# One stationary operand for two products in a recurrence kernel, and its odd heads two partition quarters away

## The chip, the cores and the metric

The kernel runs on one core of a Trainium2 chip. A core has TensorE (PE in the profile; its weight loads are listed as PEld), VectorE (DVE), ScalarE (ACT), GpSimd (POOL), SyncE (SP, which here only issues DMAs) and 16 DMA engines. Its on-chip memory has 128 partitions. TensorE is an array of 128x128; a matmul with a small operand can be placed on a part of it, called a square below: the row block is given by the partitions that the operands stand on, the column block by the partitions that the result goes to.

The metric is the device time of one execution in microseconds (us). All times below are in us where nothing else is said.

## The reference

The first half is a recurrence per batch and head over 768 time steps (4 batches, 8 heads, head size 40). The second half is a small network on the result: a matmul, x times cos(x), a matmul.

```python
for t in range(S):
    kt, vt, rt = (k[:, :, t], v[:, :, t], r[:, :, t])
    wt, at, bt = (w[:, :, t], a[:, :, t], b[:, :, t])
    y[:, :, t] = np.einsum('bhd,bhde->bhe', rt, state)
    Sa = np.einsum('bhde,bhe->bhd', state, at)
    state_decay = state * wt[:, :, None, :] - np.einsum('bhd,bhe->bhde', Sa, bt)
    state = state_decay + np.einsum('bhd,bhe->bhde', vt, kt)
...
h = x @ w_in          # (3072 x 320) @ (320 x 2048)
g = h * np.cos(h)
return g @ w_out      # (3072 x 2048) @ (2048 x 320)
```

## The kernel before, in words

**Tiling.** Time is cut into 24 chunks of 32 steps. 4 batches x 32 steps fill the 128 partitions: batch i of a chunk stands on partitions 32i to 32i+31, `blk[i]`, a quarter. Eight heads are handled as four pairs j with an even and an odd member e. Transposed operands (`aT`, `bT`, `kT`, `vT`, `rT`) hold the head dimension of an even head on partitions 0 to 39 and of an odd one on 64 to 103, `half[e]`.

**The recurrence in a chunk.** Within a chunk the steps are solved at once. Products of b (divided by the running decay) with a, masked to earlier steps, form a triangular 32x32 matrix per batch and head; its inverse is `rt`. Products of k (scaled alike) with a, masked with `su`, are `ag`. Products of v with r, plain and masked, go beside v into `vvm`. The state is kept in `qz`.

The work of a chunk is written as functions, each of which uses one or two PSUM buffers from a pool of two (`at`):
- ahead of the chunk, for pairs of chunks: `p1_w` (transposes w, makes the decays, divides b by w), `p1_a` (transposes and scales a), `p1_b` (transposes b of two chunks), `p1_n` (`nps`: the products of b with a of two chunks, 64 matmuls of 32 columns, then two copies by ACT into `nt`);
- for groups of four chunks, the inverse: a transpose on VectorE (line 486), 31 steps of two VectorE operations (lines 494 and 498) and a transpose back into `rt` (line 502), 33 entries in all;
- one chunk ahead: `p2_v` (transposes v and r), `p2_k` (transposes k), `p2_g` (`gram`: 32 matmuls for k with a, then 32 for v with r, then masks);
- the chain from chunk to chunk, called t, q, x, s, z: `ch_t` transposes the state, `ch_q` multiplies r with it, `ch_x` makes `x0ps` (32 matmuls of `ag` with `vvm`, then 32 of `aT` with `qz`), `ch_s` multiplies by the inverse (`sps`, 32 matmuls), `ch_z` makes `dps` from `kn` with `vvm` and from `bn` with the result of s, and brings the state up to date.

**Which squares these use.** In `ch_x` the first 32 matmuls of a chunk contract over quarter bb and write quarter bb ^ e: both members of every pair, eight different squares of 32x32. `ch_s` goes the other way round, on eight squares too. `p1_n` and `p2_g` use 64x32 parts, eight of them, `ch_q` four parts of 64x64, `ch_z` eight of 32x64.

**The second network** is cut into pieces for two chunks (256 tokens) and four blocks of the hidden layer. There are four kinds in turn: a and b of the first layer (`first_a`, `first_b`, tile `ph`) and two of the second layer (`second`, tile `po`). b ends in activations by ACT (lines 830 to 837) and products by VectorE (832, 840).

**Order.** Nothing is scheduled by a cost model: the order on every engine is the order in which the program issues. For each chunk a list `segs` names the functions and places M; at each M one piece of the second network is issued. Every element of the list, and every piece, is a step. With each step a counter of delayed work (`later(n, ...)`) runs down, by which DMAs, copies on POOL and the rest of the activations are issued n steps later, and one entry of the inverse is issued if any are waiting (`fill`). If the inverse is not complete when s comes up, more pieces are issued, each with four entries of the inverse, until it is. For chunk numbers that are 0, 1, 2 and 3 modulo 4 the lists are:

```python
segs = [t, v, M, q, M, k, x, M, g, M, s, pb, M, z, M, pn, M, M]
segs = [t, M, pw, q, M, x, k, M, s, v, M, z, M, pa, M, g, M, M]
segs = [t, M, pb, q, M, pn, v, M, x, M, s, k, M, g, M, z, M, M]
segs = [t, M, pw, q, M, x, k, M, s, v, M, z, M, pa, M, g, M, M]
```

The inverse for the next four chunks is put in the queue after pn of 2.

**DMA.** SP issues the loads of a chunk's inputs (four DMAs of 40 KB for each, `load`), the store of a chunk's result `xd`, and its return `xT` in the layout of the second network, three steps or more after z. SP's queue is in order.

Of the kernel before, what the change touches and what calls it, by code (L numbers as in the profile page):

```python
# [10 lines left out]
I32 = mybir.dt.int32  # L11
# [9 lines left out]
def kernel(  # L21
# [56 lines left out]
    every = slice(0, P)  # L78

# [114 lines left out]
    su = kept("su", [P, HH, C], 1, 1.0)[0]  # L194
    for i in range(4):
        nc.gpsimd.affine_select(
            su[blk[i]], su[blk[i]], pattern=[[0, HH], [1, C]], compare_op=ALU.is_gt, fill=0.0,
            base=0, channel_multiplier=-1,
        )
# [21 lines left out]
    WID = 512  # L221
    first_done, second_done = [], []

    def rounded(m, dst, src, by, by_sb):
# [16 lines left out]
        def taken():  # L241
            hi = t["words"][:, :, 1]
            t["mant"] = sb2.tile([P, WID], I32, tag="mant", name="mant")
            t["expo"] = sb2.tile([P, WID], I32, tag="expo", name="expo")
# [5 lines left out]
            t["sign"] = sb2.tile([P, WID], mybir.dt.bfloat16, tag="sign", name="sign")  # L250
# [142 lines left out]
    def over_w(c, wn):  # L393
        rw = ring.tile([P, H, D], F32, tag="rw", name="rw")
        nc.vector.reciprocal(rw, wn)  # L395
        nc.gpsimd.tensor_tensor(unpad(bn_b[c % 7]), unpad(nat["b", c]), rw, ALU.mult)  # L396
        G["rw", c] = rw

# [39 lines left out]
    def p1_n(c):  # L438
# [36 lines left out]
        if c % 4 == 2 and c > 2:  # L475
            inv_space()
# [115 lines left out]
    def p2_kn(c):  # L592
        nc.gpsimd.tensor_tensor(unpad(kn_b[c % 2]), nat["k", c], G["rw", c], ALU.mult)
        nc.gpsimd.tensor_copy(vvm[c % 2][:, :, C : C + D], nat["v", c])
        landed(c)
# [23 lines left out]
    def p2_g(c):  # L619
        kT, vT, aT, rT = G["kT"], G["vT"], G["aT", c], G["rT", c]  # L620
        ps = at("gram")
        for j in range(4):
# [6 lines left out]
        for j in range(4):  # L629
# [6 lines left out]
        ag = sb2.tile([P, H, C], F32, tag="ag", name="ag")  # L636
        nc.vector.tensor_tensor(
            ag.rearrange("p (e j) t -> p e (j t)", e=2), ps[:, :, : HH * C],
            su.rearrange("p j t -> p (j t)").unsqueeze(1).to_broadcast([P, 2, HH * C]), ALU.mult,
        )  # L640
        v1 = ps[:, :, HH * C : 2 * HH * C].rearrange("p e (j t) -> p e j t", t=C)
# [3 lines left out]
            su.unsqueeze(1).to_broadcast([P, 2, HH, C]), ALU.mult,  # L645
        )
        G["ag", c] = ag
# [28 lines left out]
    def ch_x(c):  # L676
        ps = at("x0ps")
        for j in range(4):
            o = C * (j // 2)
            for bb in range(B):  # L680
                for e in range(2):
                    mm(
                        ps[blk[bb ^ e], e, j * N72 : (j + 1) * N72], G["ag", c][blk[bb], 4 * e + j, :],
                        vvm[c % 2][blk[bb], 2 * j + e, o : o + N72], j == 0,
                    )
        if c:
            for j in range(4):
                o = (NZ - N72) * (j // 2)
                for bb in range(B):
                    for e in range(2):  # L690
                        mm(
                            ps[blk[bb ^ e], e, j * N72 : (j + 1) * N72],
# [480 lines left out]
```

## Time and profile before

| | |
|---|---|
| median of 3 runs | 800.21 (799.5 to 800.78) |
| profiled execution, its own time | 800.58 |
| its span | 798.9 |
| VectorE, time in the inverse's steps (lines 494 and 498) | 48.5 and 51.2 |
| POOL, of which the products kn (line 593) and bn (line 396) | 22.7 and 19.9 |
| DMA, mean over the span | 70 GB/s |
| TensorE idle, largest entries: wn for a scan by VectorE, bT for bn, wT for a load | 5.3, 4.9, 4.2 |

The waits in the last row lie in the first third of the execution. A row of the order in time gives start, duration, engine, line, operation, output and inputs, the tile shape of a matmul, the shape of the moving operand and how many instructions were merged. All matmuls from the helper `mm` show line 101, so they are told apart by their tiles. A duration of a merged row of matmuls includes the latency of the last one; the time that a block holds TensorE is read from its start to the next block's start.

### The profile page before, as it was taken

To read this page: it belongs to the slowest core of one execution; us is meant where nothing else is said; L and a number is where in the kernel's file an instruction comes from. 1 tells how busy PE (TensorE), PEld (TensorE's weight loads), DVE (VectorE), ACT (ScalarE), POOL (GpSimd) and SP (SyncE) were. 2 spreads that over 40 slices of the span, in tenths; PEclk is the share of its full clock that TensorE was granted. 3 is DMA by queue.
4 is the path that set the end of the run, shared out by engine and by line. 5 is a ranking of instruction groups with operands and counts; after the bars stand their busy time and mean duration, and the time that the engine had idled before them with its cause. 6 is when DMAs were issued, how large, how long until landed. Compare 5 with 4: busy or idle time off the path is not lost.

```text
span 798.9 us, 39602 instructions
## 1 busy us (share of the span) xinstructions
PE 745.9 (93%) x17812; PEld 571.0 (71%) x17812; DVE 486.7 (61%) x1025; ACT 383.4 (48%) x723; POOL 199.9 (25%) x354
## 2 busy tenths in 40 slices
PE   4768798999999999999999999999999999999997
PEld 4535576777766777777777787777787777777775
DVE  8768858864734896554895645994346863323331
ACT  1336567564435436545535635534545445354352
POOL 5326635230321330330330230332031122201000
PEclk9888899999999999999999999999999999999999
DMA  8575563343353314334214324223220222001000
GB/s 112 150 187 140 146 152 88 60 124 64 59 122 64 67 36 65 72 99 70 60 38 66 93 43 73 46 49 68 43 46 21 46 46 55 19 18 32 20 17 16
DMA packets 183304, 55.79 MB, mean 70 GB/s; under 512 B 157152, under 2 KB 178656, under 8 KB 183136
## 3 DMA queue, kind: packets, MB, share of 16 engines
q1 hardware_dynamic: 177440, 52.11, 30.6%
q8 instruction: 140, 2.29, 1.2%
q10 hardware_dynamic: 5440, 0.82, 0.8%
q0 software_dynamic: 256, 0.33, 0.3%
q14 instruction: 28, 0.23, 0.1%
HBM read 42.07 MB, written 11.14 MB: 67 GB/s over the span
## 4 chain that ended last, share of the span: by engine, by line
PE 65%; DVE 14%; DMA 5%; ACT 5%; issue 4%; POOL 3%; SPq 2%; DVEq 0%; ACTq 0%; POOLq 0%
PE ph L101 22%; PE po L101 20%; PE x0ps L101 3%; PE dps L101 3%; PE gram L101 3%; DVE rw L395 3%; PE vT L330 2%; PE sps L101 2%; PE qps L101 2%; PE nps L101 2%; DVE inv_tmp L494 2%; DVE inv L498 2%; DVE mant L245 1%; SPq L152 1%; PE kT L330 1%
## 5 line engine op out<-in xcount | busy, mean ns | idle before, releaser
L101 PE MATMUL po<-w_out_sb,gT 128*128 128x320 f32 x768 | 223.5, 439 | 0.1
L101 PE MATMUL ph<-xT,w_in_sb 128*128 128x256 f32 x768 | 185.7, 386 | 0.1
L101 PEld LDWEIGHTS po<-w_out_sb,gT 128*128 128x128 f32 x768 | 140.2, 190 | 54.6 <-issue 2.3
L101 PEld LDWEIGHTS ph<-xT,w_in_sb 128*128 128x128 f32 x768 | 139.3, 190 | 29.7 <-issue 12.4
L830 ACT ACTIVATE turns<-ph,rnd 128x512 f32<-128x512 f32 x96 | 64.1, 685 | 156.3 <-PE ph L101 155.9
L832 DVE SCALAR_TENSOR_TENSOR turns<-turns,ph 128x512 f32<-128x512 f32 x96 | 64.0, 683 | 109.4 <-ACT turns L830 109.2
L840 DVE TENSOR_TENSOR gT<-ph,turns 128x512 f32<-128x512 f32 x96 | 65.8, 686 | 38.4 <-ACT turns L837 38.4
L756 POOL TENSOR_TENSOR qz<-qz,wc 128x160 f32<-128x160 f32 x92 | 41.9, 475 | 168.5 <-DVE qz L755 167.9
L837 ACT ACTIVATE turns<-turns,half_pi 128x512 f32<-128x512 f32 x96 | 69.3, 722 | 3.1
L836 ACT ACTIVATE turns<-turns 128x512 f32<-128x512 f32 x96 | 60.1, 626 | 19.0 <-DVE turns L832 19.0
L101 PE MATMUL ph<-xT,w_in_tail 64*128 64x256 f32 (+1 forms) x512 | 54.6, 394 | 1.6 <-issue 1.6
L498 DVE TENSOR_TENSOR inv<-inv,inv_tmp 128x31 f32<-128x31 f32 (+15 forms) x124 | 51.2, 413 | 4.3
L755 DVE TENSOR_TENSOR qz<-dps,qz 128x160 f32<-128x160 f32 x92 | 28.9, 314 | 37.6 <-PE dps L101 37.3
L586 POOL COPY vp<-nat_v 128x320 f32<-128x320 f32 x24 | 11.7, 487 | 159.9 <-DMA nat_v<-in_v_dram 139.6
L494 DVE TENSOR_TENSOR inv_tmp<-u,inv 128x31 f32<-128x31 f32 (+15 forms) x124 | 48.5, 391 | 2.3
L395 DVE RECIPROCAL rw<-nat_w 128x320 f32<-128x320 f32 x20 | 42.8, 2142 | 0.1
L101 PEld LDWEIGHTS ph<-xT,w_in_tail 64*128 64x128 f32 (+1 forms) x512 | 32.2, 160 | 10.8 <-issue 7.3
L767 POOL TENSOR_TENSOR yt<-yt,wb 128x512 f32<-128x512 f32 x24 | 31.6, 1318 | 22.1 <-DVE yt L762 22.1
L659 ACT COPY s<-sT 104x416 f32<-104x416 f32 x46 | 20.8, 503 | 33.1 <-PE sT L655 33.1
L719 DVE TENSOR_TENSOR sm<-sps,su 128x128 f32<-128x128 f32 x48 | 11.7, 285 | 33.1 <-ACT sm L714 30.3
L396 POOL TENSOR_TENSOR bn<-nat_b,rw 128x320 f32<-128x320 f32 x22 | 19.9, 905 | 44.3 <-DVE rw L395 44.2
L671 ACT COPY qz<-qps 40x512 f32<-40x512 f32 x46 | 26.6, 579 | 6.8 <-PE qps L101 6.4
(136 smaller groups left out, 1100.3 us busy)
## 6 DMA issues: line engine op xcount, KB each, us to landing
words<-in_moe_w_in_dram SPq DMA_DIRECT2D x8, 512.0 KB
xd<-yt SPq DMA_DIRECT2D x48, 80.0 KB
out_dram<-ot SPq DMA_DIRECT2D x24, 160.0 KB
nat_k<-in_k_dram SPq DMA_DIRECT2D x92, 40.0 KB
nat_v<-in_v_dram SPq DMA_DIRECT2D x92, 40.0 KB
nat_r<-in_r_dram SPq DMA_DIRECT2D x92, 40.0 KB
nat_a<-in_a_dram SPq DMA_DIRECT2D x84, 40.0 KB
ws<-in_w_dram SPq DMA_DIRECT2D x5, 640.0 KB
```

The lines of the kernel that those rows point to most:

```text
L101: nc.tensor.matmul(o, lhsT=lhsT, rhs=rhs, start=start, stop=stop, skip_group_check=True)
L395: nc.vector.reciprocal(rw, wn)
L494: nc.vector.tensor_tensor(tmp, u[:, j : j + 1, :j].to_broadcast([P, C - j, j]), x[:, j:, j : j + 1].to_broadcast([P, C - j, j]), ALU.mult,)
L498: nc.vector.tensor_tensor(x[:, j:, :j], x[:, j:, :j], tmp, ALU.subtract)
L755: nc.vector.tensor_tensor(z, pick(dp, 0, (2 * N72 + C, 2), (N72, 2), (1, D)), z, ALU.add)
L756: nc.gpsimd.tensor_tensor(z, z, wc.rearrange("p (f m b) -> p f m b", f=2, m=2)[:, :, :, bb] .unsqueeze(3).to_broadcast([P, 2, 2, D]), ALU. ...
L767: nc.gpsimd.tensor_tensor(yt.rearrange("p j b t -> p (j b) t"), yt.rearrange("p j b t -> p (j b) t"), wx, ALU.mult)
L830: nc.scalar.activation(n, u, ACTF.Identity, bias=rnd, scale=1.0)
L832: nc.vector.scalar_tensor_tensor(n, n, -ROUND, u, ALU.add, ALU.subtract)
L836: nc.scalar.activation(n, n, ACTF.Abs)
L837: nc.scalar.activation(n, n, ACTF.Sin, bias=half_pi, scale=-2.0 * math.pi)
L840: nc.vector.tensor_tensor(gT[:, 2 * e : 2 * e + 2].rearrange("p f t -> p (f t)"), us[e], ns[e], ALU.mult)
```

## The change

From chunk 8 on (`QT = 8`):

- k and b of one chunk are transposed into one PSUM buffer (`p1_kb`) and copied into one tile `kb`, in which the 32 columns of k and the 32 of b of a batch and head stand side by side, in turned order for every other batch. `p1_kn` multiplies these 64 columns at once with a: 32 matmuls a chunk, on 64x64 parts, give both the product of b (to `nt`) and that of k (masked into `ag`), on neighbouring quarters. The four quarters are taken out of PSUM by four ACT copies and four VectorE masks.
- So `p2_k` and the k half of `p2_g` go. k is needed earlier: a second load of k into `ke` (`early_k`) and its product with 1/w into `kne` (`early_kn`).
- The results of an odd head come out two quarters away from those of its batch. `spot` gives the quarter p on which `ag`, `vvm`, `kn` and `bn` of batch bb and member e stand, and g = p ^ 1 for the inverse. In x0ps (shown in the diff; sps and dps are changed in the same way) the contraction is over p and the result goes to g; in sps the reverse. To bring k, b and v of odd heads to their quarter, POOL copies or multiplies in three parts (`placed`): even heads, and the odd heads of either half of the partitions.
- `kb`, `ke`, `kne` and two of the five `ag` tiles share memory (`cv`) with the scratch tiles of the weights' rounding, which ends before. The mask `su` loses its head dimension.
- The lists change (the last four lines of the diff, again for 0, 1, 2 and 3 modulo 4); nps is made for one chunk at a time, and the inverse is queued after the fourth.

```diff
+    def spot(c, bb, e):
+        p = bb ^ 2 * e
+        return (p, p ^ 1) if c >= QT else (bb, bb ^ e)
...
+    def placed(c, dst, x, by=None):
+        lo, hi = slice(0, P // 2), slice(P // 2, P)
+        parts = [(every, every, slice(0, H, 2)), (lo, hi, slice(1, H, 2)), (hi, lo, slice(1, H, 2))]
+        for to, of, h in parts if c >= QT else [(every, every, slice(0, H))]:
+            if by is None:
+                nc.gpsimd.tensor_copy(dst[to, h], x[of, h])
+            else:
+                nc.gpsimd.tensor_tensor(dst[to, h], x[of, h], by[of, h], ALU.mult)
...
+    def early_k(c):
+        for i in range(B):
+            nc.sync.dma_start(
+                ke[blk[i]], src["k"][i, :, c * C : (c + 1) * C, :].rearrange("h t d -> t h d")
+            )
+    def early_kn(c):
+        placed(c, unpad(kne), ke, G["rw", c])
+        if c + 1 < NCH:
+            later(1, lambda: early_k(c + 1))
+    def p1_kb(c):
+        ps = at("kbT")
+        turned(ps[:, 0], kne)
+        turned(ps[:, 1], bn_b[c % 7])
+        for i, o, n in ((0, 0, 3 * C), (1, C, C)):
+            nc.scalar.copy(
+                pick(kb, o, (4 * C, 2 * B), (n, 2), (1, C)),
+                pick(ps[:, i], 0, (2 * C, 2 * B), (C, 2), (1, C)),
+            )
+        if c % 2 == 0:
+            later(3, lambda: early_kn(c + 1))
+    def p1_kn(c):
+        ps = at("nps")
+        for j in range(4):
+            for x in range(2):
+                for m in range(2):
+                    for e in range(2):
+                        p = 2 * m + x
+                        bb = p ^ 2 * e
+                        mm(
+                            ps[slice(m * DP, (m + 1) * DP), e, (4 * x + j) * C : (4 * x + j + 1) * C],
+                            pick(kb[half[e]], (j * B + p) * DP, (1, DP)), G["aT", c][half[e], j, blk[bb]],
+                            j == 0 and x == 0,
+                        )
...
+        for g in range(B):
+            for x, to, put in (
+                (1 - g % 2, G["nt"][blk[g], :, c % 4].rearrange("p t e j -> p e j t"), nc.scalar.copy),
+                (g % 2, ag[blk[g]].rearrange("p (e j) t -> p e j t", e=2), None),
+            ):
...
     def p2_kn(c):
-        nc.gpsimd.tensor_tensor(unpad(kn_b[c % 2]), nat["k", c], G["rw", c], ALU.mult)
-        nc.gpsimd.tensor_copy(vvm[c % 2][:, :, C : C + D], nat["v", c])
+        placed(c, unpad(kn_b[c % 2]), nat["k", c], G["rw", c])
+        placed(c, vvm[c % 2][:, :, C : C + D], nat["v", c])
...
     def p2_g(c):
...
+        if c >= QT:
+            for j in range(4):
+                for bb in range(B):
+                    for e in range(2):
+                        mm(
+                            ps[blk[spot(c, bb, j % 2)[0]], e, j * C : (j + 1) * C],
+                            vT[half[e], j, blk[bb]], rT[half[e], j, blk[bb]], j == 0,
+                        )
+            first_v(c, ps[:, :, : HH * C])
+            return
...
+                    p, g = spot(c, bb, e)
                     mm(
-                        ps[blk[bb ^ e], e, j * N72 : (j + 1) * N72], G["ag", c][blk[bb], 4 * e + j, :],
-                        vvm[c % 2][blk[bb], 2 * j + e, o : o + N72], j == 0,
+                        ps[blk[g], e, j * N72 : (j + 1) * N72], G["ag", c][blk[p], 4 * e + j, :],
+                        vvm[c % 2][blk[p], 2 * j + e, o : o + N72], j == 0,
                     )
...
+                segs = [t, v, M, q, M, x, M, g, M, s, kb0, M, z, M, kn0, M, M]
+                segs = [t, M, pw, q, M, x, kb1, M, s, v, M, z, M, pa, M, kn1, M, g, M]
+                segs = [t, M, kb2, q, M, kn2, v, M, x, kb3, M, s, M, kn3, M, z, M, g, M]
+                segs = [t, M, pw, q, M, x, M, s, v, M, z, M, pa, M, g, M, M]
```

In chunks 20 to 23, in which nothing is made ahead any more, the list is the old one without k.

## The prediction

> **What bounds the kernel now.** I read the busy shares first, then the busy time of single chunks of the steady part, then the order in time on TensorE, and last the groups of weight loads.
>
> ```profile
> PE   745.9 (93%) x17812; PEld 571.0 (71%) x17812; DVE 486.7 (61%) x1025; ACT 383.4 (48%) x723; POOL 199.9 (25%) x354
> ```
>
> The stretches below are chunks 10 and 11 (columns: span, then busy time and count of PE, weight loads, DVE, ACT, POOL, then granted clock).
>
> ```profile
> 359.00:388.00 29.00, 29.00 (x760) 22.61 (x758) 15.30 (x39) 15.15 (x29) 4.36 (x8) 1.00 0.35 62
> 388.00:417.00 29.00, 28.29 (x638) 22.14 (x637) 27.80 (x57) 11.34 (x22) 9.16 (x17) 1.00 0.23 48
> ```
>
> From chunk 8 on TensorE has no idle time to speak of, at a full clock. Its time is the kernel's time. Only in every fourth chunk (7, 11, 15), where the inverse runs on VectorE, is another engine level with it: DVE 27.80 of 29.00, with 0.71 of TensorE idle.
>
> So the question is how long each block of small matmuls holds TensorE. The order in time gives it, from the start of one block to the start of the next (start, duration, engine, instruction, count). Each f32 matmul shows as two records.
>
> ```profile
> 441.05 1.29 PE L101 MATMUL nps<-aT,bT 40*32 40x32 f32 x128
> 442.27 4.57 PE L101 MATMUL po<-w_out_sb,gT 128*128 128x320 f32 x16
> 446.68 0.88 PE L655 MATMUL sT<-ident,qz 104*104 104x104 f32 x8
> ...
> 450.12 0.82 PE L101 MATMUL qps<-rT,s 40*40 40x32 f32 x64
> 450.75 1.07 PE L101 MATMUL ph<-xT,w_in_tail 64*64 64x256 f32 x16
> 451.75 1.99 PE L101 MATMUL ph<-xT,w_in_sb 128*128 128x256 f32 x8
> 453.68 0.88 PE L101 MATMUL x0ps<-vvm,ag 32*32 32x72 f32 x64
> 454.49 0.89 PE L101 MATMUL x0ps<-qz,aT 40*32 40x72 f32 x64
> 455.30 0.66 PE L330 MATMUL kT<-ident,kn 128*128 128x128 f32 x4
> 458.05 0.88 PE L101 MATMUL sps<-x,rt 32*32 32x72 f32 x64
> 458.86 0.66 PE L330 MATMUL vT<-ident,vp 128*128 128x128 f32 x4
> 469.15 0.73 PE L101 MATMUL gram<-aT,kT 40*32 40x32 f32 x62
> 469.72 0.73 PE L101 MATMUL gram<-rT,vT 40*32 40x32 f32 x62
> 470.38 4.57 PE L101 MATMUL po<-w_out_sb,gT 128*128 128x320 f32 x16
> ```
>
> Four things are to be seen.
> - On the full array 16 records of 320 columns take 446.68 - 442.27 = 4.41, so a column takes 4.41 / (16 x 320) = 0.86 ns.
> - The tail of ph uses four squares of 64x64. 16 records of 256 columns take 451.75 - 450.75 = 1.00. One square gets four of them: 4 x 256 x 0.86 = 0.88. So **one square streams a column no faster than the whole array, and the gain is only that squares run beside each other**. What counts is how many different squares a block uses.
> - The gram block has two halves of 64 records in the same array shape. The first gives way after about 0.54, the second, followed by full-array work, only after 0.68 (469.70 to 470.38). Leaving a shape costs about 0.14.
> - x0ps and sps take 0.81, that is 0.67 plus 0.14. A record of 72 columns needs 72 x 0.86 = 62 ns on its square. Their 64 records lie on eight squares (row block bb, column block bb^e), eight on each: 0.50. So they are not limited by the squares now.
>
> The weight loads get longer with the number of stationary columns (32, 40, 64, 128): mean 103, 118, 134, 190 ns, about 0.9 ns a column on top of some 75.
>
> ```profile
> L101 PEld LDWEIGHTS po<-w_out_sb,gT 128*128 128x128 f32 x768 | 140.2, 190 | 54.6 <-issue 2.3
> L101 PEld LDWEIGHTS x0ps<-vvm,ag 32*32 32x32 f32 x1536 | 17.1, 103 | 8.7 <-issue 5.7 <-ACT turns L837 1.8 <-ACT turns L836 0.4
> L101 PEld LDWEIGHTS qps<-rT,s 40*40 40x40 f32 x1472 | 16.3, 118 | 6.9 <-issue 3.1 <-ACT s L659 2.3 <-ACT rT L611 1.0
> L101 PEld LDWEIGHTS ph<-xT,w_in_tail 64*64 64x64 f32 x256 | 9.9, 134 | 1.1
> ```
>
> qps has the shape that the new nps will have: four squares of 64x64, 32 moving columns, 64 records. It takes 450.75 - 450.12 = 0.63, 16 records a square, 39 ns each. 32 moving columns need only 28 ns; 40 stationary columns at 0.86 need 34. So qps looks bound by its weight loads, plus some 5 ns.
>
> **The change part by part.** All of it lies in chunks 8 to 23, sixteen chunks.
>
> Removed on TensorE: the k half of gram. 64 records a chunk at 0.54 = -0.54, on the bound engine: 16 x 0.54 = **-8.6**. The transposes of k move but stay as many: four of k and four of b a chunk, now in one block; 0.
>
> nps: one block of 128 records for two chunks (442.27 - 441.05 = 1.22, 0.61 a chunk) becomes one of 64 for each chunk, 64 stationary columns on four squares. Lower end: as fast as qps, 0.63, plus 0.14 for leaving the shape (qps is followed by its own shape) = 0.77. Upper end: 64 x 0.86 + 5 = 60 ns a record, 16 a square, 0.96 + 0.14 = 1.10. The weight-load rows speak for the upper end; I take 58 ns, 1.07: +0.46 x 16 = **+7.4**. Eight more blocks also make the block ahead of each leave its shape: 8 x 0.14 = **+1.1**.
>
> The Trainium skill, TensorE: Matmul & The Clock Gate, section LDWEIGHTS, says that a load's time goes by the columns, columns / 1.2, whatever the contraction. By it a load of 64 takes an estimated 53 ns, and nps would come to 0.85 + 0.14 = 0.99, 1.3 us less in the sum than I take.
>
> x0ps and sps: this is where I see the price. With p = bb ^ 2e and g = p ^ 1 the first half of x0ps goes from row block p to column block p^1, for both e. These are four squares, (0,1), (1,0), (2,3), (3,2), where there were eight. sps likewise. Each square gets 16 records of 62 ns: 0.99, plus 0.14 = 1.13, against 0.81: +0.32. That is the lower end if a square's time binds. The order is A B C D B A D C; where a matmul must wait for its square and all behind it wait too, eight matmuls (two records of 62 each, 13 ns between issues) take 0.274 rather than 0.248, and a block 4 x 0.274 + 0.14 = 1.24: +0.43. The bottom end, if a square does not bind, is 0. I take the middle of the two upper values, 0.37, since the tail of ph shows the square's rate outright: 0.37 x 2 blocks x 16 = **+11.8**. The other half of x0ps, dps, qps and the v half of gram still use as many squares as before.
>
> Inverse: one of its 33 entries is issued with each step of the plan. Before, it starts after pn early in chunk c%4==2, and the last entry is issued at q of the next c%4==0, seven steps ahead of s. These (q, b, k, x, two of the second layer, g) hold 0.6 + 2.9 + 0.5 + 1.6 + 4.4 + 1.2 = 11 us of TensorE. After, it starts only after kn3, some ten steps later, and the last two entries are forced out in the very step ahead of s. So the cover goes. From the start of that chunk VectorE must do ten steps (by the groups of lines 494 and 498, sizes 220 down to 31: 7.7 us), the final transpose (1.96), and about 5.0 of L832, L840, copies and masks: 14.7. TensorE needs about 15.8 up to s (t 0.7, v 1.0, q 0.6, x 2.0, g 0.7, first-layer pieces 6.4, second-layer ones 4.4). So rt comes about in time if VectorE has no backlog, and 0 to 3 us late if it has. Four places (8, 12, 16, 20): 0 to 12, I take 0.25 each, **+1.0**.
>
> Masks and copies of nps: four copies by ACT of 0.62 a chunk where there was half of two, four DVE masks of 0.42 where there was one (+30 us of ACT, +20 of DVE over the run). ACT has 15 of 29 busy and DVE 15 where they fall; they hide behind the pieces of the second network. The tight place is kn2, v, one piece, x in c%4==2: the copies queue behind the activations of the piece ahead, vT's and rT's copies behind them, and x and kb3 need these buffers. 0 to 1.2 in each of four chunks; I take 0.25, **+1.0**.
>
> POOL: three operations for one in bn, kn, vvm, and three for the new kne; by halves of the rows of L396, L593 and L594, +0.45, +0.47, +0.26, +1.4 = 2.6 us a chunk, 9.16 of 29 at most now. It is not short of time, but VectorE pays: beside POOL's bn (394.84 to 395.75) a DVE step takes 0.96 where its like takes 0.42.
>
> ```profile
> 395.07 0.96 DVE L498 TENSOR_TENSOR inv<-inv,inv_tmp 128x252 f32<-128x252 f32 x1
> ...
> 396.52 0.42 DVE L498 TENSOR_TENSOR inv<-inv,inv_tmp 128x255 f32<-128x255 f32 x1
> ```
>
> In c%4==3 that is up to +3 on an engine at 27.80, less 0.42 for the mask that left and 0.7 for smaller steps; the 0.71 that TensorE idles there now works the other way. I take 0 for both together, with -2 to +6 as ends.
>
> The second load of k (four DMAs a chunk, some 2 us of SP's queue, as nat_k takes now) waits on POOL's kne, and behind it stand the loads of later chunks. The return of xT is issued ahead of it. xT's way to the piece after t gets one piece shorter in c%4==1 (about 6.0 to 4.8 us from its issue); it has landed by about 472 where it is used at 475.5, so it stays hidden: 0, at most 1 x 3. Scratch tiles shared with the rounding of the weights: their waits are the same ones, 0.
>
> Sum: -8.6 + 7.4 + 1.1 + 11.8 + 1.0 + 1.0 = +13.7. The profiled execution took 800.58 (span 798.9), 0.4 above the median of 800.21. 800.6 + 13.7 = **814**.
>
> **The rivals.**
> - *A square is not the limit* (faster). If two records can follow each other on a square at the pace of issue, x0ps and sps keep 0.81, nps takes 0.77: -8.6 + 2.6 + 1.1 = -4.9, **796**. For it: the small blocks run at 8 to 10 ns a record, which is issue. Against: the tail of ph. It decides from the point where the 48 touched blocks grow by less than (8.6 - 1.1) / 48 = 0.16 each.
> - *Weights of 64 columns load unseen*: nps 0.77, the rest as forecast, 814 - 4.8 = **809**. For it: dps with 64 stationary columns takes no longer a record than sps. Against: that has eight squares.
> - *VectorE becomes the bound* around the inverse: 3 us at each of the four places more, **825**. For it: 27.80 of 29.00 and the lost 11 us; against: 15 of 29 busy in the chunk before.
>
> **How the numbers follow.** Forecast 0.60, weights unseen 0.13, VectorE 0.11, squares not binding 0.16. About 0.2% is what a measurement can tell from no change. Faster 0.14, same 0.02 (both from the first rival), slower 0.84. The forecast's own ends are -8.6 + 10.2 + 2.6 + 0.8 = +5 (806) and -8.6 + 13.8 + 7.8 + 2.5 + 9 = +24.5 (825), the 9 for waits, whose ends (12, 4.8 and 6) will hardly meet. A range of 804 to 824 leaves out the first rival and the top of the third.
>
> **What would show it.** Right: x0ps's first half and sps 1.1 to 1.25 to the next block, nps about 1.07, gram's remaining half about 0.68, chunks 20 to 23 longer than 26.7 although a block was taken out of them. Wrong: these blocks still at 0.81; or TensorE idle ahead of sps for rt, which would put the loss on VectorE. The weakest terms are nps (one shape, extrapolated from 40 to 64 columns) and the wait for rt.

## The result, and the profile after

The changed kernel takes **871.95** (median of 4, 869.02 to 875.61), the kernel before beside it 800.5 (799.5 to 801.53): a ratio of 1.088 (95%: 1.085 to 1.091). The change costs 71.5, where the forecast said 13.7. The profiled execution took 875.61, the longest of the four; its span is 873.8, and the span before was 798.9. These two spans differ by 74.9, and the trace's account below is of that.

The busy shares after, from the profile page:

```profile
PE 779.0 (89%) x16772; PEld 594.2 (68%) x16772; DVE 508.0 (58%) x1073; ACT 417.5 (48%) x771; POOL 256.2 (29%) x499
```

TensorE has 1040 records less and is busy for 33 us more. The rest of the loss is idle: 74.9 - 33.1 = 42. The mean granted clock (the share of full speed that the profile shows for TensorE) fell from 0.983 to 0.953 over the span, and a lower clock is part of the longer busy time too.

The order in time on TensorE first, since the forecast was made of it (start, duration, engine, line, instruction; in brackets the idle time ahead of a row, and what ended it):

```profile
404.88 1.14 PE L107 MATMUL nps<-aT,cv 40*64 40x32 f32 x64
405.94 0.66 PE L344 MATMUL vT<-ident,vp 128*128 128x128 f32 x4
...
411.29 1.20 PE L107 MATMUL x0ps<-vvm,ag 32*32 32x72 f32 x64 [2.10 <-DVE cv L550]
412.42 1.06 PE L107 MATMUL x0ps<-qz,aT 40*32 40x72 f32 x63
...
420.57 1.20 PE L107 MATMUL sps<-x,rt 32*32 32x72 f32 x64
421.70 1.99 PE L107 MATMUL ph<-xT,w_in_sb 128*128 128x256 f32 x8
...
429.24 0.80 PE L107 MATMUL dps<-vvm,kn 32*64 32x72 f32 x52 [1.20 <-DVE ag L550]
```

From block to block, x0ps's first half and sps take 1.13 (412.42 - 411.29, 421.70 - 420.57), nps 1.06. These are the forecast's block prices. What it does not have stands in the brackets: 2.10 idle ahead of x0ps and 1.20 ahead of dps, both for VectorE's mask of nps (line 550). One more such wait, of 2.4, stands ahead of sT of chunks 10, 14 and 18, and so counts to 9, 13 and 17 below.

The chunks, from one sT to the next, show where the 74.9 lies:

| chunks | before | after | difference |
|---|---|---|---|
| 5, 6 | 36.0, 30.5 | 53.1, 45.2 | +31.8 |
| 7, 11, 15 | 28.9, 29.1, 29.3 | 27.2, 27.8, 27.8 | -4.5 |
| 8, 12, 16 | 29.7, 29.7, 30.3 | 32.1, 31.8, 31.9 | +6.1 |
| 9, 13, 17 | 28.1, 28.1, 28.1 | 32.0, 33.0, 31.9 | +12.6 |
| 10, 14, 18 | 28.8, 28.9, 30.4 | 39.7, 36.4, 35.6 | +23.6 |
| 19 to 22 | 21.9, 26.7, 26.7, 26.8 | 21.8, 36.0, 21.6, 26.4 | +3.7 |

Pieces of the second network move as well: chunks 8, 12 and 16 have eight full-array records of ph more (about 2 us), which 9, 13 and 17 lack, and chunk 20 has 16 records of po more, which 21 lacks. So the rows are best read together. In chunks 7, 11 and 15 VectorE is no longer level with TensorE, and they got shorter. Over 40% of the loss sits in 5 and 6; of the rest most is in the chunks with two nps (10, 14, 18). Chunks 5 and 6 belong to the change: k, b and nps of chunks 8 to 11 are made there, from lists of their own.

**The first cause: ACT and VectorE read nps in turn.** The way of one nps out of PSUM, on both engines (the eight operations begin with the first and end with the last row):

```profile
406.91 0.57 ACT L548 COPY nt<-nps 32x256 f32<-32x256 f32 x1
407.52 0.41 DVE L550 TENSOR_TENSOR cv<-nps,su 32x256 f32<-32x256 f32 x1 [1.06 <-ACT nt L548]
407.96 0.59 ACT L548 COPY nt<-nps 32x256 f32<-32x256 f32 x1 [0.48 <-DVE cv L550]
408.58 0.42 DVE L550 TENSOR_TENSOR cv<-nps,su 32x256 f32<-32x256 f32 x1 [0.66 <-ACT nt L548]
...
410.71 0.43 DVE L550 TENSOR_TENSOR cv<-nps,su 32x256 f32<-32x256 f32 x1 [0.65 <-ACT nt L548]
```

Each mask waits for the copy ahead of it, and each copy for the mask. So the eight take 411.14 - 406.91 = 4.23: their sum, not the longer of two columns (four copies of 0.58 are 2.3). All that time they hold one of the two PSUM buffers of `at`, and x0ps waits for it. Over the run the list of waits has four entries for it, none of which was there before (who waited, for what: us in total, times, longest):

```profile
DVE ag L550 <- ACT nt L548: 28.0, 34, 3.0
DVE cv L550 <- ACT nt L548: 23.9, 27, 2.6
...
ACT nt L548 <- DVE ag L550: 15.0, 27, 1.4
...
ACT nt L548 <- DVE cv L550: 11.1, 21, 1.4
```

The kernel before has the same trait, where one PSUM tile is read by both engines. Its list of instruction groups shows it (busy, mean ns, then idle time ahead and what ended it):

```profile
L642 ACT COPY vvm<-gram 128x256 f32<-128x256 f32 x24 | 8.8, 368 | 42.6 <-DVE ag L637 42.3
L697 DVE COPY x<-x0ps 128x288 f32<-128x288 f32 x24 | 11.0, 456 | 26.1 <-ACT x L696 26.1
```

**The second: POOL's queue in chunk 5 (and 6).** POOL and TensorE there:

```profile
208.64 2.47 POOL L421 TENSOR_TENSOR bn<-nat_b,rw 128x160 f32<-128x160 f32 x3 [1.52 <-DVE rw L409]
211.17 0.45 POOL L662 COPY vp<-nat_v 128x320 f32<-128x320 f32 x1
211.56 0.46 POOL L662 COPY rp<-nat_r 128x320 f32<-128x320 f32 x1
211.98 1.81 POOL L421 TENSOR_TENSOR cv<-cv,rw 128x160 f32<-128x160 f32 x3
213.84 1.12 PE L344 MATMUL kbT<-ident,cv 128*128 128x128 f32 x4 [4.55 <-POOL cv L421]
```

TensorE waits 4.55 for kne (`cv` here), the last row of POOL. POOL's queue itself starts late at that place: it was idle 1.52 for VectorE's `rw`. In chunk 6 TensorE waits 4.91. But the masks of nps cost these two chunks as much: x0ps, vT and dps wait 9.3 for line 550 there.

**The third: rt**, on the chain that ended last (start, duration, what):

```profile
479.54 1.96 DVE rt L578
481.50 0.14 issue
481.63 1.20 PE sps L107 x64
```

sps waits for it 0.4 in each of chunks 8, 12 and 16, and 3.71 in chunk 20.

**And the clock.** Chunks 10, 11, 14 and 18 by their stretches (span, then busy time and count of PE, weight loads, DVE, ACT, POOL, then granted clock):

```profile
396.20:436.00 39.80, 35.00 (x697) 27.09 (x698) 14.01 (x31) 19.60 (x36) 6.09 (x12) 0.88 0.30 52
436.00:463.80 27.80, 27.80 (x569) 21.66 (x568) 25.91 (x56) 11.03 (x21) 13.11 (x29) 1.00 0.24 51
528.70:565.10 36.40, 32.61 (x696) 25.23 (x697) 13.92 (x31) 19.56 (x36) 6.00 (x12) 0.95 0.33 56
656.70:692.30 35.60, 32.30 (x756) 25.14 (x756) 15.50 (x36) 19.51 (x36) 7.45 (x16) 1.00 0.17 35
```

Chunks 10, 14 and 18 have the same list and the same waits for masks (2.4 ahead of sT, 2.1 ahead of x0ps, 1.2 ahead of dps). Chunk 10 takes 3.4 more than 14 with the same records, at a clock of 0.88 rather than 0.95, and 4.2 more than 18, at full clock, which even has 60 records more (matmuls of one column that pad it, as before). Before, each chunk from 8 on ran at a granted clock of 1.00.

In all traces here the granted clock is either 1.00 or 0.50. In each trace the stretches at 0.50 start whole multiples of 3.41 apart, and they last 3.41 or a multiple of it (but for the last, which the end of the trace cuts off). Chunk 10 has 0.50 from 395.87 to 399.28 and from 412.94 to 419.76, chunk 14 from 528.99 to 532.40, chunk 18 nowhere. In such a stretch the records of po start every 0.53, at full clock every 0.27. The stretches of 3.41 before these three, and below them the two of chunk 14 in which x0ps waits:

```profile
392.46:395.87 3.41, 1.36 (x67) 0.81 (x65) 1.43 (x5) 1.99 (x4) 3.07 (x8) 1.00 0.28 45
409.52:412.94 3.42, 1.65 (x114) 1.58 (x119) 2.23 (x4) 2.85 (x6) 0.00 (x0) 1.00 0.53 85
525.58:528.99 3.41, 0.99 (x68) 0.90 (x69) 1.69 (x4) 1.89 (x4) 3.13 (x7) 1.00 0.15 25
539.23:542.64 3.41, 2.49 (x12) 1.50 (x9) 1.25 (x3) 1.96 (x5) 0.00 (x0) 1.00 0.54 85
542.64:546.06 3.42, 2.25 (x130) 2.07 (x131) 1.81 (x3) 3.34 (x7) 0.00 (x0) 1.00 0.52 85
```

Where a wait lies wholly or mostly within one stretch, as in the first three rows, TensorE is busy for 0.99 to 1.65 of it, and the next is at half clock. Where the same wait lies across the border of two, as in the last two rows, the clock stays; so it does in chunk 18 (busy for 2.39 and 2.03 around sT, for 2.48 and 2.25 around x0ps). Over all traces here, chunks 5 to 22, a stretch at full clock with less than 0.4 of it busy was always followed by one at half clock, one with more than 0.7 never, and in between both came. So it was in part luck that chunk 10 lost more than 18.

### The profile page after: what moved, and what is told of

It is laid out like the page before. It is cut to its first block, busy times and chain, and to the rows that moved or that the text cites. A ratio compares the mean times of both kernels' runs of the same rounds, so it can differ in the third digit from the quotient of the medians.

```text
span 873.8 us, 37895 instructions
## 1 busy us (share of the span) xinstructions
PE 779.0 (89%) x16772; PEld 594.2 (68%) x16772; DVE 508.0 (58%) x1073; ACT 417.5 (48%) x771; POOL 256.2 (29%) x499
## 4 chain that ended last, share of the span: by engine, by line
PE 61%; DVE 17%; ACT 9%; issue 5%; DMA 4%; POOL 2%; SPq 1%; POOLq 0%; DVEq 0%; ACTq 0%
PE ph L107 21%; PE po L107 17%; PE x0ps L107 4%; PE dps L107 4%; ACT nt L548 4%; PE sps L107 3%; PE kbT L344 2%; DVE rw L409 2%; PE vT L344 2%; PE qps L107 2%; DVE ag L550 2%; PE nps L107 2%; DVE cv L550 1%; ACT turns L929 1%; PE gram L107 1%
## 5 line engine op out<-in xcount | busy, mean ns | idle before, releaser
L107 PE MATMUL po<-w_out_sb,gT 128*128 128x320 f32 x768 | 232.2, 449 | 1.5 <-issue 1.5
L107 PE MATMUL ph<-xT,w_in_sb 128*128 128x256 f32 x768 | 190.4, 393 | 3.3 <-issue 3.3
L107 PEld LDWEIGHTS po<-w_out_sb,gT 128*128 128x128 f32 x768 | 143.3, 195 | 57.7 <-issue 8.0
L107 PEld LDWEIGHTS ph<-xT,w_in_sb 128*128 128x128 f32 x768 | 143.2, 195 | 35.3 <-issue 15.5
L548 ACT COPY nt<-nps 32x256 f32<-32x256 f32 x64 | 37.6, 587 | 43.6 <-PE nps L107 17.5
L570 DVE TENSOR_TENSOR inv_tmp<-u,inv 128x31 f32<-128x31 f32 (+15 forms) x124 | 51.5, 416 | 1.9
L574 DVE TENSOR_TENSOR inv<-inv,inv_tmp 128x31 f32<-128x31 f32 (+15 forms) x124 | 49.3, 397 | 4.3
L847 DVE TENSOR_TENSOR qz<-dps,qz 128x160 f32<-128x160 f32 x92 | 28.6, 311 | 28.8 <-PE dps L107 28.7
L810 DVE TENSOR_TENSOR sm<-sps,su 128x128 f32<-128x128 f32 x48 | 11.7, 285 | 55.0 <-ACT sm L805 46.6
L421 POOL TENSOR_TENSOR bn<-nat_b,rw 64x160 f32<-64x160 f32 (+2 forms) x54 | 31.4, 582 | 39.7 <-DVE rw L409 22.3
L859 POOL TENSOR_TENSOR yt<-yt,wb 128x512 f32<-128x512 f32 x24 | 31.9, 1328 | 22.8 <-DVE yt L854 22.8
L107 PEld LDWEIGHTS sps<-x,rt 32*32 32x32 f32 x1536 | 23.5, 109 | 17.6 <-issue 13.9
```

What stands on the lines that cost most here:

```text
L107: nc.tensor.matmul(o, lhsT=lhsT, rhs=rhs, start=start, stop=stop, skip_group_check=True)
L548: put(to, of)
L570: nc.vector.tensor_tensor(tmp, u[:, j : j + 1, :j].to_broadcast([P, C - j, j]), x[:, j:, j : j + 1].to_broadcast([P, C - j, j]), ALU.mult,)
L574: nc.vector.tensor_tensor(x[:, j:, :j], x[:, j:, :j], tmp, ALU.subtract)
```

## The experiments

Theory after the first look: the blocks cost about what was forecast, and the rest is the way of nps out of PSUM, POOL's queue in chunks 5 and 6, and rt. Rivals: the four squares cost far more than their block times say (a matmul that waits for its square holding up all behind it), or moving the odd heads does.

### Four squares alone, in two orders

The kernel before, with nothing changed but where the results go: x0ps and sps on four squares, visited A B C D or A A B B. The change itself is A B C D B A D C.

```diff
-            for bb in range(B):
-                for e in range(2):
+            for e in range(2):
+                for bb in range(B):
                     mm(
-                        ps[blk[bb ^ e], e, j * N72 : (j + 1) * N72], G["ag", c][blk[bb], 4 * e + j, :],
+                        ps[blk[bb ^ 1], e, j * N72 : (j + 1) * N72], G["ag", c][blk[bb], 4 * e + j, :],
```

(The results of nps and sps follow; in the second kernel the two loops stay as they were.)

> The kernel before with one thing changed: in x0ps (first half) and sps both members of a pair go from quarter bb to bb ^ 1, so four squares in place of eight, visited in the order A B C D. Theory that a square's stream binds (62 ns a record of 72 columns): both blocks 1.13 in place of 0.81, 47 blocks (24 sps, 23 or 24 x0ps) x 0.32 = +15, 815. Rival, squares do not matter and another trait of the changed kernel made its blocks long: 800 to 802.

> As sq4_abcd, but the four squares are visited A A B B C C D D. If only the sum of a square's time counts: 815 again, blocks 1.13. If a matmul waiting for its square holds up those behind it: blocks about 2.3, 47 x 1.5 = +70, 871.

Measured: 809.99 for A B C D, ratio 1.012 (1.009 to 1.016), +10.6; 813.09 for A A B B, ratio 1.015 (1.011 to 1.019), +13.7. The order in time of the first:

```profile
457.72 1.20 PE L101 MATMUL x0ps<-vvm,ag 32*32 32x72 f32 x64
458.85 0.89 PE L101 MATMUL x0ps<-qz,aT 40*32 40x72 f32 x64
```

and of the second:

```profile
460.18 1.27 PE L101 MATMUL x0ps<-vvm,ag 32*32 32x72 f32 x64
461.38 0.83 PE L101 MATMUL x0ps<-qz,aT 40*32 40x72 f32 x61
```

A block takes 1.13 and 1.20, against 0.81 on eight squares. So the price is the sum of a square's records. Two matmuls in a row on one square add only 0.07; the rival with long stalls falls. 47 blocks by 0.32 would be 15; 10.6 came out. From chunk 5 to 22 of the first kernel's trace TensorE is busy for 11.8 more (36 blocks by 0.32 are 11.5) and idle for 3.5 less, so part of the price is hidden in waits that were there already (chunk 11, where VectorE is level with TensorE, takes 29.1, as before).

### A wider stationary operand alone

The kernel before, with qps's stationary operand made 64 columns (zeros beyond 40) and all else the same, on the same four squares.

```diff
-                        ps[half[e], f, i * C : (i + 1) * C], G["s"][half[f], i, half[e]],
+                        ps[full[e], f, i * C : (i + 1) * C], G["s"][half[f], i, full[e]],
```

> The kernel before with one size changed: the stationary operand of qps has 64 columns (24 of them zero) in place of 40, on the same four squares with the same 32 moving columns. Theory that weight loads bind four squares: 64 records at 16 x 58 ns, the block 0.63 to about 0.95, 23 blocks: +7, 807. Rival, that 64 columns load unseen and nps is long because of its shape change alone: 800 to 801.

Measured: 803.68 (median of 9), ratio 1.006 (1.003 to 1.008), +4.1, where 807 (+7) was expected. Its order in time:

```profile
448.14 1.14 PE L101 MATMUL qps<-rT,s 40*64 40x32 f32 x64
449.09 1.07 PE L101 MATMUL ph<-xT,w_in_tail 64*64 64x256 f32 x16
```

The block takes 0.95 where it took 0.63, with the same moving columns, so weight loads set its pace: (0.95 - 0.63) / 16 records = 20 ns for 24 columns, 0.83 ns a column. The rule that the prediction cites (the Trainium skill, TensorE: Matmul & The Clock Gate, section LDWEIGHTS: columns / 1.2) gives 20 ns for them too. For a whole record of 64 columns it gives 53, and 59 are measured here (0.95 / 16). The second rival, weights that load unseen, falls.

### The way of nps out of PSUM

One copy and one mask over all partitions, in place of four and four. This leaves the quarters unsorted: those of odd batches hold the other product, so the kernel serves to show times alone.

```diff
-        for g in range(B):
-            for x, to, put in (...):
-                ...
+        nc.scalar.copy(G["nt"][:, :, c % 4].rearrange("p t e j -> p e j t"), part[0])
+        nc.vector.tensor_tensor(
+            ag.rearrange("p (e j) t -> p e j t", e=2), part[1], pick(su, 0, (0, 2), (0, HH), (1, C)), ALU.mult
+        )
```

> The changed kernel with nps taken out of PSUM by one ACT copy and one VectorE mask over all partitions in place of four of each; the quarters of odd batches get the other product, so the result is not the reference's. Theory that the alternation of ACT and VectorE over nps makes the loss (each of the eight waits for the one before, 4.1 us a chunk): the waits of x0ps, dps and sT for it (2.1 in five chunks, 1.2 in four, 2.4 in three, 22 us) and the clock lost behind them (some 10) go: 835 to 845. Rival, that the loss lies in POOL's queue and the inverse: above 860.

Measured: 834.23, ratio 1.045 (1.039 to 1.051), just below the expected range: **37.7 less than the change**. Its order in time:

```profile
243.44 0.61 ACT L542 COPY nt<-nps 128x256 f32<-128x256 f32 x1 [0.87 <-PE nps L107]
244.08 0.42 DVE L543 TENSOR_TENSOR cv<-nps,su 128x256 f32<-128x256 f32 x1 [0.79 <-ACT nt L542]
244.56 0.65 PE L344 MATMUL vT<-ident,vp 128*128 128x128 f32 x4 [0.17 <-DVE cv L543]
```

The two still go in turn, but an operation on 128 partitions takes no longer than one on 32, so nps is out in 1.06 instead of 4.2. The waits of x0ps, dps and sT for these masks are gone. Chunk 10, by its stretch, takes 30.6 at full clock instead of 39.7 at 0.88:

```profile
379.50:410.10 30.60, 30.60 (x708) 23.98 (x697) 11.49 (x25) 16.16 (x31) 8.28 (x17) 1.00 0.40 72
```

The second kernel keeps the eight operations and issues the four copies first, then the four masks.

> The changed kernel with the same eight operations on nps issued as four ACT copies and then four VectorE masks, so one hand-over in place of seven. Theory that what counts is when nps's buffer comes free (the sum of all eight, 4.1 us, since the engines never read it at once): the waits of x0ps (2.1), dps and sT stay, only ACT comes free 1.7 us earlier: 862 to 872. Rival, that the hand-overs and the engines' idling between them make the loss: 835 to 845, as with wide.

Measured: 858.85, ratio 1.075 (1.071 to 1.078). Its order in time:

```profile
397.19 2.39 ACT L552 COPY nt<-nps 32x256 f32<-32x256 f32 x4
399.61 1.72 DVE L554 TENSOR_TENSOR cv<-nps,su 32x256 f32<-32x256 f32 x4 [2.88 <-ACT nt L552]
```

4.14 against 4.23: fewer handovers shorten it little; its length is the eight durations. x0ps still waits 1.9 to 2.4 and dps 1.1, as expected, while sT's wait falls from 2.4 to 1.4. The rival, 835 to 845, falls. But the total is 13.1 less than the change and 3 below the expected range, with a clock of 0.969 rather than 0.953. In the trace, from chunk 5 to 22, TensorE is busy for 8.9 less and idle for 7.7 less than in the change's; why the clock is better is not shown. The first mask reads a quarter whose copy ended some 1.8 earlier, and still starts only when the last copy ends.

The Trainium skill, PSUM — Partial Sum Buffer, section "PSUM bank collisions raise a hardware error", says that two engines must not access one bank in the same quarter of the partitions at once, reads against reads included, while different quarters do not collide. All traces here agree with the first half: no copy of nps overlaps with a mask of it. By the second half the copy of one quarter could run beside the mask of another; in the program as built these too wait for each other. A kernel that lets them run side by side was not tried, so no run here shows the second half.

### The odd heads left in place

Odd heads stand on their own quarter, and POOL works in one part instead of three. The results of both members then fall on the same square, in the order A A B B.

```diff
-        p = bb ^ 2 * e
+        p = bb
...
-        for to, of, h in parts if c >= QT else [(every, every, slice(0, H))]:
+        for to, of, h in [(every, every, slice(0, H))]:
...
-                        bb = p ^ 2 * e
+                        bb = p
```

> The changed kernel with odd heads left on their own quarter (p = bb for both members, g = p ^ 1; POOL's copies and products in one part again). Each square of x0ps and sps is then visited twice in a row (A A B B C C D D); four squares as in the changed kernel. Theory that a square's total time counts and not the order of visits: both blocks stay at 1.13, POOL's queue gets shorter (kbT in chunks 5 and 6 waits some 2 us less each), 858 to 872. Rival, that a matmul which must wait for its square holds up all behind it: a block takes about 2.3 (four of eight visits wait 124 ns), +1.2 in 32 blocks, about 905.

Measured: 863.75, ratio 1.081 (1.078 to 1.084), 8.2 less than the change. The blocks are at 1.20 (0.07 longer, 32 blocks: about 2.2 in favour of moving), so an estimate of what the move costs elsewhere is about 10, part of it by the clock (0.964 in the trace rather than 0.953). kbT waits 2.88 and 3.06 for kne instead of 4.55 and 4.91. The rival, blocks of 2.3 because a waiting matmul holds up all behind it, falls here as well.

### kb and kn later in chunks 5 and 6

The changed kernel, with only these two lists changed: kb and kn of chunk 5 stand one or two places later, and in chunk 6 kb stands behind q, and v ahead of kn.

```diff
-                    t, M, kb0, q, M, kn0, k, M, x, M, s, S6, M, kb1, z, M, S7, M, kn1, pw, v, M, g, pa, M,
+                    t, M, q, M, kb0, k, M, kn0, x, M, s, S6, M, kb1, z, M, S7, M, kn1, pw, v, M, g, pa, M,
...
-                    segs.insert(segs.index(s) + 1, k)
+                    segs = [t, M, q, M, kb2, v, M, kn2, x, M, kb3, s, k, M, kn3, M, z, M, g, M]
```

> The changed kernel with the lists of chunks 5 and 6 alone altered: kb and kn stand one to two places later, behind q and the next piece. Theory that POOL's queue (bn in three parts, vp, rp, kne in three) holds up kbT there by 4.5 and 4.9: both waits go, and the clock lost behind them: 872 - 9.4 - 3 = 860. If the wait only moves to kn or x: above 868.

Measured: 856.53, ratio 1.073 (1.068 to 1.078), 15.4 less than the change. The waits of kbT fall to 1.01 and 1.17, and chunks 5 and 6 to 45.8 and 36.2, 16.3 less in all. The waits of kbT account for 7.3 of it. But x0ps no longer waits for the masks there either, where it waited 2.54 and 2.10, and the two chunks have 10.2 at half clock in place of 23.9. So the edit does not take away POOL's queue alone, and its 15.4 are not the price of that queue. The kernel's mean clock rises from 0.953 to 0.964. Chunk 10, which the edit leaves alone, takes 35.7 in this trace instead of 39.7, at 0.95 instead of 0.88.

### Together, with and without a faster inverse

The wide copy and mask, the odd heads in place and the later lists, without anything at the inverse. (This kernel was run after the next one, which its expectation speaks of.)

> As wide_nomove_late, but the inverse goes on with one entry a step (the doubled pace made VectorE the bound in every fourth chunk: 32.9 of 34.5 busy, and vT then waited 4.8). Wide nps copies (result not the reference's), odd heads not moved, later kb and kn in chunks 5 and 6. From the chunks of the runs so far (chunks 5 and 6 as in wide_nomove_late, 72; the others as in wide and nomove): about 819. Should the forecast's terms (squares, 64 columns, the wait for rt) not be all that is left, above 826.

Measured: 824.98, ratio 1.032 (1.028 to 1.035), 47 less than the change. This is 6 above the expected 819 and just below the 826 that would have spoken for another cause. One by one the three edits gave 37.7, 8.2 and 15.4, together 61: they take away partly the same waits and the same loss of clock. What is left above the kernel before is 25.7 by the medians (before 799.33 beside it), and 20 in the trace, whose execution was the shortest of its four. From chunk 5 to 22 the trace is 21.9 longer than before. TensorE is busy for 14.5 of that: the blocks account for -8.6 + 7.3 + 1.1 + 12.4 (32 blocks at 1.20) = about 12, and 3.4 at half clock for some 1.7. It is idle for the other 7.4, of which sps's waits for rt are 4.8 (3.70 of it in chunk 20). So the forecast's terms, with rt's wait at its measured size, cover nearly all that is left.

The same kernel with two entries of the inverse a step in chunks 3 modulo 4, so that rt is early:

```diff
+            if c > 5 and c % 4 == 3:
+                fill = (2, 4)
```

> The changed kernel without every cause of a wait that the traces showed: wide nps copies (result not the reference's: odd batches get the other product), odd heads not moved, kb and kn one place later in chunks 5 and 6 (so that kbT does not wait 4.5 and 4.9 for POOL's kne), and two entries of the inverse a step in every fourth chunk. If the rest of the loss is the squares and the 64 columns, what remains is -8.6 + 7.3 (nps 1.065) + 1.1 + 12.4 (x0ps and sps at 1.13 to 1.20) = +12: 812 to 816. If another cause is still hidden: above 822.

Measured: 853.74, ratio 1.067 (1.064 to 1.070): 28.8 worse than with one entry a step, and above the 822 that stood for one more cause. Here it is: chunk 11 by its stretch:

```profile
406.90:441.40 34.50, 30.12 (x570) 23.24 (x569) 32.88 (x78) 10.13 (x19) 7.80 (x16) 0.95 0.19 40
```

and TensorE's order in time just behind it:

```profile
441.38 0.88 PE L740 MATMUL sT<-ident,qz 104*104 104x104 f32 x8
447.07 1.09 PE L344 MATMUL vT<-ident,vp 128*128 128x128 f32 x4 [4.82 <-DVE vvm L729]
```

VectorE is busy 32.88 of 34.50, and TensorE waits for it. sps no longer waits for rt in chunks 8 to 20, but steps pulled forward take VectorE's time where it has none. This is the forecast's third rival, brought about by this edit.

### Sorting the quarters outside PSUM

Two wide masks by VectorE bring all of nps out, the first into `ag`, the second into spare columns of `cv`; ACT copies and POOL copies then sort the quarters between on-chip tiles. With odd heads in place and the later lists, and first with two entries of the inverse a step:

```diff
+        both = [ag, cv[:, 2368 : 2368 + H * C].rearrange("p (h t) -> p h t", t=C)]
+        for x in range(2):
+            nc.vector.tensor_tensor(both[x]..., ps[:, :, 4 * x * C : 4 * (x + 1) * C]..., pick(su, ...), ALU.mult)
+        for g in (1, 3, 0, 2):
+            nc.scalar.copy(G["nt"][blk[g], :, c % 4]..., both[1 - g % 2][blk[g]]...)
+        for g in (1, 3):
+            nc.gpsimd.tensor_copy(ag[blk[g]], both[1][blk[g]])
```

> As wide_nomove_late, but with the right result: two VectorE masks over all partitions take nps out of PSUM (0.85 us), and the odd quarters are sorted afterwards out of on-chip memory, off PSUM (four ACT copies to nt, two POOL copies within ag). If it is the PSUM buffer that counts, about as fast as wide_nomove_late, 812 to 820; if the number of operations on ACT counts wherever they read, 830 to 840.

Measured: 863.71, ratio 1.081 (1.077 to 1.085), above both expected ranges; vT waits 4.8 for VectorE in chunks 8, 12 and 16, as in the kernel just shown. With one entry a step:

> As cure, with the right result, and one entry of the inverse a step: 819 plus what four ACT copies and two POOL copies off PSUM cost: 820 to 832.

Measured: 835.5, ratio 1.045 (1.042 to 1.048), 3.5 above the expected range; kbT now waits 0.9 to 1.1 in chunks 10, 14 and 18, for what the trace does not show. It takes 36 less than the change, but 4.5% more than the kernel before. None of these kernels is faster than the kernel before.

### Zero matmuls where TensorE waits

To price the lower clock by itself, matmuls of zeros were put ahead of x in chunks 5, 6, 10, 14 and 18, and ahead of kb in 5 and 6.

```diff
+                if c in (5, 6, 10, 14, 18) and seg is x:
+                    kept_busy(24)
+                if c in (5, 6) and i == 2:
+                    kept_busy(52)
```

> The changed kernel with matmuls of zeros put where TensorE waits longest: 24 of them (1.9) ahead of x in chunks 5, 6, 10, 14 and 18, 52 (4.2) ahead of kb in chunks 5 and 6. The waits stay. If the lower granted clock behind the waits costs time of its own (0.87, 0.89, 0.88 and 0.95 in chunks 5, 6, 10 and 14), some 10 to 14 us come back: 858 to 862. If the clock costs nothing: 872 to 874.

Measured: 891.35, ratio 1.117 (1.113 to 1.120), 19 worse than the change and outside both expected ranges. Its order in time:

```profile
407.61 2.32 PE L107 MATMUL po<-w_out_sb,gT 128*128 128x320 f32 x8
414.30 3.68 PE L107 MATMUL po<-idle 128*128 128x192 bf16 x24 [4.37 <-ACT ot L957]
417.91 1.20 PE L107 MATMUL x0ps<-vvm,ag 32*32 32x72 f32 x64
```

The zero matmuls write into spare columns of po, and so wait 4.37 themselves for ACT's copy of po; then they take 3.7. So the run cannot tell what the clock costs. That is read from the records that start every 0.53 instead of every 0.27, and from chunks 10, 14 and 18: 39.7, 36.4 and 35.6 at 0.88, 0.95 and 1.00.

## Why the prediction was wrong

The sign was right; the size was wrong by 58, and 871.95 lies far outside 804 to 824. By its own steps:

- *gram, nps, the leaving of a shape.* Right. gram's half is left at 0.69, nps takes 1.065 where 1.07 was taken, and the 64-column run shows that the stationary columns set it. (The 469.70 of the prediction is 469.72 in its row, where each half lacks two records. The ends of its range take 0.8 and 2.5 for terms that it does not spell out; nothing turned on them.)
- *x0ps and sps.* Right in mechanism and nearly in size: +0.32 a block, the lower end; the middle value 0.37 allowed for stalls in order that did not show. TensorE's four terms come to -8.6 + 7.3 + 1.1 + 10.2 = +10.0, against the forecast's +11.7.
- *Masks and copies of nps, "they hide behind the pieces of the second network", +1.0.* **This step failed**, and it is the largest part: TensorE waits 26.3 for the masks (x0ps 10.9, sT 7.2, dps 4.8, vT 3.4), and taking the eight operations down to two gives 38 back. The forecast compared what ACT and VectorE have to do with what time they have. It did not ask how long the eight together hold a PSUM buffer, and priced the two engines apart. They take turns, 4.2 for one nps, and that begins 0.97 after the block behind nps has started. In the stretch shown x0ps could have started at 409.19, where the piece ahead ends (406.87 + 2.32); the buffer comes free at 411.14.
- *POOL, "It is not short of time", 0.* This failed too, as an argument from an average: where kne is wanted in chunks 5 and 6 it stands behind bn in three parts, vp and rp, and TensorE waits 9.5 for it. The later lists give 15 back and leaving the odd heads in place 8, but each takes away other waits or lost clock as well. The forecast's only worry on POOL, that VectorE pays in 3 modulo 4, did not come: VectorE has 25.9 busy in chunk 11, less than the 27.8 before.
- *"All of it lies in chunks 8 to 23".* Not so. Chunks 5 and 6, where the work for 8 to 11 is made ahead, have 31.8 of the 74.9. The forecast gave them no row.
- *Inverse.* The step was right, 0 to 12 its ends, +1.0 the value taken, about 5 the measured wait: 3 times 0.42, and 3.71 at chunk 20. It stays (3.9 in chunk 20) where nps leaves PSUM in two operations.
- *SP, xT.* 0 holds as far as seen: no wait for xT is among TensorE's larger ones.
- *A full clock* was taken for granted. It held before in every chunk from 8 on. After, from chunk 5 to 22, 41.0 are at half clock, and TensorE is busy in 35.7 of them. If half of that is lost, an estimate from the records that start every 0.53 instead of 0.27, the lower clock costs some 18.
- *Rivals.* A square that is not the limit: fallen (1.13). Weights of 64 columns unseen: fallen (0.95 in qps). VectorE as the bound: not in the changed kernel, but shown to be close, by the runs with two entries of the inverse a step.
- *Signs.* Block times were a good sign. "Chunks 20 to 23 longer than 26.7" was a poor one: pieces move between chunks, and 21 and 22 took 21.6 and 26.4. One sign of being wrong came, TensorE idle ahead of sps for rt, but with 3.71 at most it is a small part.

How much is waiting and how much the clock can be read from the traces. From sT of chunk 5 to sT of chunk 23, with what TensorE does in that time:

| kernel | length | busy | idle | at half clock | of it busy |
|---|---|---|---|---|---|
| before | 517.8 | 508.8 | 9.0 | 0 | 0 |
| the change | 591.4 | 538.9 | 52.5 | 41.0 | 35.7 |
| odd heads in place | 581.0 | 533.7 | 47.2 | 23.9 | 23.9 |
| four copies, then four masks | 574.8 | 530.0 | 44.8 | 20.5 | 17.7 |
| later kb and kn | 574.0 | 534.6 | 39.3 | 27.3 | 25.3 |
| one copy, one mask | 551.6 | 527.9 | 23.7 | 20.5 | 17.2 |
| the three edits together | 539.7 | 523.3 | 16.4 | 3.4 | 3.4 |

The change adds 73.6 here. Idle time is 43.5 of it: 26.3 for the masks of nps, 9.5 for kne (1.5 for POOL's bn before), 5.0 for rt, and small waits. Busy time is 30.1: 10.0 for the blocks, some 18 for the clock, and 2 not taken apart. So the four squares and the 64 columns cost what was forecast, and what failed is that all else would hide. The clock's share is an estimate, and it differs from one execution to the next: the four of the changed kernel have mean clocks from 0.953 to 0.964.

## What to carry to other kernels

When a result in PSUM is taken out by two engines, price the time until the buffer is free, and look in the profile for rows in which one engine waits for the other on the same tile; where they do, as here, that time is the sum of all their operations. Split by partitions, an operation cost as much as a whole one here, so four quarters cost four times. And follow a change to where its first inputs are made ahead, chunks earlier: POOL, busy for 29% of the span, was still late there.

## What was not expected of the hardware

- A mask of 32x256 takes 0.42 and one of 128x256 0.42, a copy 0.59 and 0.61. On POOL a product takes 0.52 for 64x160, and 0.86 for 128x320 with four times the elements. These are groups of line 421 after (count, min/median/max in ns, first and last start, shapes):

```profile
L421 POOL TENSOR_TENSOR bn<-nat_b,rw x54: 516/522/1169, 13.2 to 653.2; 64x160 f32<-64x160 f32 x32, 128x160 f32<-128x160 f32 x16, 128x320 f32<-128x320 f32 x6
L421 POOL TENSOR_TENSOR bn<-w_out_sb,rw x2: 856/859/862, 21.1 to 26.2; 128x320 f32<-128x320 f32 x2
```

- Two matmuls in a row on the same square (A A B B) cost only 0.07 a block more than A B C D.
- Waits of 2.1 to 2.4 on TensorE were followed by a stretch of 3.41 or more at half clock in chunks 10 and 14 where they lay wholly or mostly within one such stretch (TensorE busy for 0.99 to 1.65 of it), and by none in 14 and 18 where they lay across two (busy for 2.03 to 2.49 of each).
